# One decay sum made from the other on VectorE from step 3 on, with all instruction orders drawn up anew, in a fused RWKV6 and squared-ReLU kernel

## The chip, the cores and the metric

The kernel runs on one core of a Trainium2 chip. The metric is the device time of one execution in microseconds. Before the change three runs took 183.56, 183.57 and 184.78 us; the median is 183.57.

The engines are named as in the profile: PE is TensorE (matrix products), PEld its weight loads, DVE is VectorE, ACT is ScalarE, POOL is GpSimd, SP is SyncE, which here only issues DMAs. SBUF is the on-chip memory; PSUM is the accumulator memory into which PE writes and which DVE and ACT can read.

## The reference

A recurrence per batch and head, over 768 time steps, then a feed-forward part over its 3072 output rows. Cut to what matters:

```python
# r, k, v, w: (4 batches, 8 heads, 768 steps, 48); u: (8, 48); w_in: (384, 2048); w_out: (2048, 384)
for t in range(S):
    cur = einsum('bhd,bhe->bhde', u[None] * kt, vt)
    y[:, :, t] = einsum('bhd,bhde->bhe', rt, state + cur)
    state = wt[:, :, :, None] * state + einsum('bhd,bhe->bhde', kt, vt)
x = y.transpose(0, 2, 1, 3).reshape(B * S, H * D)      # (3072, 384)
h = x @ w_in
r = maximum(h, 0.0)
out = (r * r) @ w_out
```

## The kernel before

**Tiling.** The 3072 rows are worked off in 12 steps, s = 0 to 11, of 256 time steps each: three per batch, so steps 0, 3, 6 and 9 begin a batch. In a step, partition p holds the time steps 2p and 2p + 1, and the two halves of 64 partitions are two chunks c = 0, 1 of the recurrence. The heads go in four pairs.

**The recurrence of a step.** `ww_` multiplies the decays of the two time steps of a partition, `lw_` takes the logarithm (ACT) into one of two buffers `lw_buf`, in bfloat16. `cum_` forms sums of these logarithms on PE as products with constant triangles: four narrow products with `half_ones` (L309) give each chunk's whole decay, one 384-column product with `tri_strict` (L311) the sum before each time step, and one with `tri_incl_neg` (L312) the negated sum up to and with it. Both 384-column sums stand in one PSUM tile `cs` of two banks, `att0` or `att1`. `exp_` (L317, ACT) takes the exponential of both in place, `ac_` that of the chunk decays. `rd_` (DVE) multiplies r by the first (L332, two instructions) and k by the second (L335); `rw_` and `kw_` have before that multiplied r and k of one of the two time steps by a decay. `tr_` transposes the two on PE and `rkt_` copies them to SBUF (steps 0 to 3), or `dtr_` transposes them by DMA (steps 4 to 11). `p_` (L385) multiplies them, `pm_` (DVE) applies a mask, `y_` (L441) multiplies with v (`vs_`, a rearranged copy; `v_` is another in bfloat16), `su_` (L412) forms the chunk's share of the state, `ts_`, `sn_` and `sb_` pass the state on, `yc_` (L441) adds what comes from the state. `ku_`, `qp_`, `q_`, `qs_` and `vq_` form the part with u, which `ysb_` (L463, DVE) adds to y. The result is transposed by PE (`yt_`) and copied (`xt_`) in steps 0 to 5, and by DMA (`dyt_`) in steps 6 to 11.

**The feed-forward part of a step.** `m1_` in eight groups (L492, 6 products of 256 columns each), each into one of two PSUM banks; `rl_` (ReLU, ACT or DVE) empties the bank; `sq_` squares two groups at a time (ACT or DVE); `m2_` (L517) in two halves of 128 rows, each four parts of four products of 384 columns; `os_` (ACT or DVE) and a store. The weights come as float32 in four pieces each (`ld.*.i`, `ld.*.o`) and are cast once (`cast`).

**The order.** There is no scheduler at run time and none at build time: a string `ORDER` lists every operation, and a loop at the end issues them one by one. The order of the words that fall to one engine is the order of that engine's queue, and each engine works its queue strictly in order, waiting at an instruction until what it reads is written and what it overwrites has been read. A word names the operation, the step, a part, the PSUM bank behind a colon and, where there is a choice, the engine behind an equals sign: `rl_.1.4=A` on ACT, `=V` on DVE, `=G` on POOL. `warm_.9.0` are nine products of a zero tile of 512 columns into a bank that nobody reads (L534), issued where PE has nothing to do in the opening. All loads, stores and DMA transposes stand in SP's queue.

Before, the opening of `ORDER` is:

```
ld.0.w ww_.0=V ld.0.k kw_.0=G lw_.0 warm_.9.0 cum_.0:0 exp_.0 rd_.0.1 warm_.8.1 tr_.0.1:0 rkt_.0.1=A ld.0.r
rw_.0=V ld.1.w ww_.1=G rd_.0.0 warm_.4.2 tr_.0.0:1 ld.0.u ku_.0=V qp_.0=V q_.0 ac_.0 lw_.1 ld.1.k ld.0.v
```

Of the kernel before, what the change touches and what calls it, by code (L numbers as in the profile page):

```python
# [17 lines left out]
ld.0.w ww_.0=V ld.0.k kw_.0=G lw_.0 warm_.9.0 cum_.0:0 exp_.0 rd_.0.1 warm_.8.1 tr_.0.1:0 rkt_.0.1=A ld.0.r  # L18
rw_.0=V ld.1.w ww_.1=G rd_.0.0 warm_.4.2 tr_.0.0:1 ld.0.u ku_.0=V qp_.0=V q_.0 ac_.0 lw_.1 ld.1.k ld.0.v
ld.1.r ld.1.v warm_.1.0 cum_.1:1 rkt_.0.0=A warm_.1.0 p_.0.0:m kw_.1=G ld.2.w pm_.0.0 p_.0.1:0 pm_.0.1 ku_.1=G  # L20
exp_.1 v_.0=A rd_.1.1 rw_.1=G qp_.1=V ld.2.i warm_.7.0 su_.0:m vs_.0.1=A ts_.0.0=A ld.1.i vs_.0.0=A qs_.0=A
ld.0.i sn_.0.0 warm_.5.0 y_.0:0 tr_.1.1:0 sb_.0.0=A warm_.2.1 yc_.0 vq_.0=G ww_.2=G ts_.0.1=V rd_.1.0
rkt_.1.1=V vs_.1.0=A v_.1=A warm_.1.2 tr_.1.0:1 ysb_.0=V lw_.2 rkt_.1.0=V warm_.4.2 yt_.0:0 sn_.0.1 sb_.0.1=A
ac_.1 vs_.1.1=G q_.1 qs_.1=G p_.1.1:0 p_.1.0:m vq_.1=G cast.i.2=A cast.i.1=A xt_.0=V pm_.1.0 su_.1:b ts_.1.0=V
cum_.2:1 sn_.1.0 pm_.1.1 cast.i.0=G m1_.0.4:0 m1_.0.5:1 sb_.1.0=A y_.1:0 yc_.1 ts_.1.1=V rl_.0.5=V ysb_.1=V
rl_.0.4=A m1_.0.2:1 rl_.0.2=A ld.2.k m1_.0.3:0 ld.2.r kw_.2=G rl_.0.3=A exp_.2 ld.3.i yt_.1:0 sn_.1.1
m1_.0.0:1 m1_.0.1:0 cast.i.3=G ld.2.v ku_.2=V xt_.1=V rl_.0.0=A ac_.2 rl_.0.1=A m1_.1.0:1 qp_.2=G rw_.2=V
rl_.1.0=A m1_.1.1:0 rl_.1.1=A sb_.1.1=A ld.0.o m1_.1.3:1 rd_.2.0 rd_.2.1 ld.1.o rl_.1.3=V tr_.2.0:1 cast.o.0=G
tr_.2.1:0 rkt_.2.0=V m1_.1.2:0 m1_.1.6:1 rkt_.2.1=V rl_.1.2=V v_.2=A sq_.0.0=A p_.2.1:0 p_.2.0:1 q_.2 su_.2:b
ts_.2.0=V pm_.2.0 m1_.0.6:0 rl_.1.6=A sq_.0.1=A rl_.0.6=A m1_.0.7:1 rl_.0.7=A ld.2.o vs_.2.1=G vs_.2.0=G  # L30
m2_.0.0.0:0 pm_.2.1 sn_.2.0 sq_.1.0=V m1_.1.4:0 cast.o.1=A cast.o.2=V m2_.0.1.0:1 ld.3.o rl_.1.4=A qs_.2=A
m1_.1.7:1 sb_.2.0=V vq_.2=V cast.o.3=V sq_.0.2=A sq_.1.1=V ld.3.w m2_.0.1.1 m1_.1.5:0 ld.3.k ld.3.r ku_.3=G
y_.2:1 yc_.2 m2_.0.0.1 rl_.1.7=A sq_.0.3=A m2_.0.1.2 m2_.0.0.2 m2_.0.1.3 m2_.0.0.3 ww_.3=V lw_.3 ld.3.v
os_.0.1=A os_.0.0=A cum_.3:0 ysb_.2=V yt_.2:1 xt_.2=V exp_.3 ac_.3 rl_.1.5=V sq_.1.3=A sq_.1.2=A m2_.1.0.0:0
m1_.2.3:1 ld.4.w vs_.3.0=G kw_.3=V qp_.3=V m1_.2.1:0 m2_.1.0.1 rw_.3=G rl_.2.1=A v_.3=A rl_.2.3=A m2_.1.0.2
m2_.1.0.3 ww_.4=G m1_.2.5:0 rd_.3.1 su_.3:1 ld.4.r ld.4.k q_.3 vs_.3.1=A rd_.3.0 m1_.2.4:1 os_.1.0=A qs_.3=G
ts_.3.0=A sn_.3.0 rl_.2.4=V tr_.3.1:1 lw_.4 kw_.4=G tr_.3.0:0 rw_.4=G rkt_.3.1=A cum_.4:0 exp_.4 rl_.2.5=V
m1_.2.0:1 ld.4.v rl_.2.0=A m1_.2.2:0 m2_.1.1.0:1 rl_.2.2=A m2_.1.1.1 ts_.3.1=V rkt_.3.0=V sn_.3.1 rd_.4.1
ku_.4=G vq_.3=G p_.3.0:m v_.4=A ac_.4 sq_.2.2=A sb_.3.0=A rd_.4.0 pm_.3.0 ld.6.w su_.4:1 p_.3.1:0 m2_.1.1.2
m2_.1.1.3 ld.5.k pm_.3.1 m1_.2.6:0 y_.3:0 yc_.3 qp_.4=G sq_.2.1=A sq_.2.0=A m1_.2.7:1 ld.5.w os_.1.1=V  # L40
m2_.2.0.0:0 ts_.4.0=V dtr_.4.1 dtr_.4.0 sb_.3.1=A rl_.2.6=A sn_.4.0 ld.6.v ld.6.k ld.5.r ww_.5=G ysb_.3=V q_.4
yt_.3:1 m2_.2.0.1 ts_.4.1=V m2_.2.0.2 p_.4.1:0 p_.4.0:1 rl_.2.7=V sq_.2.3=V xt_.3=A m2_.2.1.0:1 vs_.4.1=A
lw_.5 m1_.3.2:0 store.1.0 m1_.3.3:1 qs_.4=G pm_.4.1 sn_.4.1 rl_.3.2=A vs_.4.0=G cum_.5:0 m1_.3.0:0 rl_.3.3=A
vq_.4=G sb_.4.0=V pm_.4.0 ac_.5 ww_.6=G m1_.3.7:1 exp_.5 m2_.2.0.3 sq_.3.1=A y_.4:1 rl_.3.0=V rl_.3.7=A yc_.4
ld.6.r rw_.6=G m1_.3.1:0 ku_.5=G qp_.5=G m1_.3.4:1 ld.7.w store.1.1 os_.2.0=A ku_.6=G m2_.2.1.1 kw_.5=V
rw_.5=V kw_.6=V rl_.3.1=A lw_.6 m1_.3.5:0 ld.5.v ysb_.4=V store.2.0 cum_.6:1 ww_.7=G ld.8.w yt_.4:0 ld.7.k
kw_.7=G rd_.5.1 rd_.5.0 xt_.4=V rl_.3.4=A sq_.3.0=A rl_.3.5=A exp_.6 m1_.3.6:1 v_.6=A m2_.2.1.2 rl_.3.6=V
m2_.3.0.0:0 m1_.4.3:0 v_.5=A m2_.2.1.3 ac_.6 su_.5:0 rd_.6.1 rd_.6.0 rl_.4.3=V dtr_.5.0 su_.6:1 ts_.5.0=V
sq_.3.2=A sb_.4.1=A dtr_.5.1 q_.5 sq_.3.3=A os_.2.1=A vs_.5.0=A lw_.7 dtr_.6.0 qs_.5=A vs_.5.1=A ld.7.v ld.7.r
m1_.4.7:1 m1_.4.5:0 rl_.4.5=V m2_.3.0.1 m2_.3.0.2 m2_.3.0.3 m1_.4.6:0 ts_.6.0=V sn_.6.0 sn_.5.0 sb_.5.0=A  # L50
ts_.6.1=V qp_.6=G vs_.6.0=G p_.5.1:0 p_.5.0:1 rl_.4.7=V m2_.3.1.0:1 m1_.4.0:1 rl_.4.6=V pm_.5.1 dtr_.6.1
sq_.4.3=A os_.3.0=A vq_.5=G m2_.3.1.1 rl_.4.0=V pm_.5.0 vs_.6.1=A cum_.7:0 m2_.3.1.2 m1_.4.1:0 y_.5:1 ac_.7
exp_.7 rl_.4.1=A sb_.6.0=A yc_.5 m1_.4.4:1 m2_.3.1.3 q_.6 sq_.4.0=A ysb_.5=V ku_.7=G qp_.7=G rw_.7=G ww_.8=G
yt_.5:0 ld.8.v ld.9.v rl_.4.4=V p_.6.1:1 m1_.4.2:0 xt_.5=V pm_.6.1 ld.9.w rd_.7.1 m1_.5.4:1 m2_.4.1.0:0 v_.7=G
rl_.4.2=A m1_.5.3:0 ld.8.k rd_.7.0 rl_.5.4=A m1_.5.7:1 rl_.5.3=A store.0.0 sn_.6.1 p_.6.0:1 rl_.5.7=V su_.7:0
ld.8.r m1_.5.5:0 ww_.9=G qs_.6=A m1_.5.6:1 pm_.6.0 q_.7 ts_.7.0=V sq_.4.1=A vq_.6=G rl_.5.6=A dtr_.7.0 lw_.8
os_.3.1=V y_.6:1 dtr_.7.1 rl_.5.5=V sn_.7.0 ts_.7.1=V vs_.7.1=G yc_.6 m2_.4.1.1 m1_.5.0:1 m2_.4.0.0:1
vs_.7.0=A rl_.5.0=A v_.9=A ld.9.r m1_.5.2:0 sq_.4.2=V ysb_.6=V kw_.8=V rl_.5.2=A dyt_.6 store.3.0 sb_.6.1=A
sb_.7.0=A cum_.8:0 m2_.4.0.1 sq_.5.1=A store.2.1 store.3.1 m2_.4.0.2 ld.9.k p_.7.0:m p_.7.1:1 pm_.7.0
m2_.4.1.2 m2_.4.0.3 m1_.5.1:0 m2_.4.1.3 m1_.6.7:1 exp_.8 pm_.7.1 qs_.7=G sn_.7.1 vq_.7=G rl_.5.1=A lw_.9  # L60
rw_.8=G rd_.8.0 rd_.8.1 os_.4.0=A m1_.6.2:0 y_.7:1 rl_.6.7=A ac_.8 yc_.7 vs_.8.1=G rl_.6.2=A v_.8=G ld.10.v
rw_.9=G dtr_.8.1 dtr_.8.0 sb_.7.1=V os_.4.1=V cum_.9:0 m1_.6.3:1 sq_.5.2=A sq_.5.0=V exp_.9 rl_.6.3=V
sq_.5.3=A sq_.6.1=A ac_.9 kw_.9=G ku_.9=G ku_.8=G qp_.8=G m1_.6.0:0 m2_.5.0.0:1 m2_.5.0.1 rl_.6.0=V ysb_.7=V
m1_.6.1:1 m1_.6.4:0 m2_.5.0.2 rd_.9.0 rl_.6.4=A rl_.6.1=V store.4.1 m2_.5.0.3 su_.8:1 rd_.9.1 su_.9:0
ts_.8.0=V sn_.8.0 p_.8.0:m dyt_.7 p_.8.1:1 pm_.8.0 m2_.5.1.0:0 ld.10.w m2_.5.1.1 m1_.7.4:0 vs_.8.0=A sq_.6.0=A
m1_.7.0:1 sb_.8.0=A os_.5.0=V q_.8 ts_.9.0=V m2_.5.1.2 m2_.5.1.3 rl_.7.4=A rl_.7.0=V pm_.8.1 m1_.7.7:0
m1_.7.2:1 y_.8:1 ww_.10=V yc_.8 ld.11.w dtr_.9.1 rl_.7.7=A qs_.8=G vq_.8=G rl_.7.2=A m1_.6.5:0 m1_.6.6:1
# [520 lines left out]
```

## Time and profile before

| | us |
|---|---|
| three runs | 183.56, 183.57, 184.78 |
| median | 183.57 |
| the profiled execution | 184.86 |
| its span, first to last instruction | 182.9 |
| outside the span | 1.96 |

| engine | busy us | share of the span | instructions |
|---|---|---|---|
| PE | 173.3 | 95% | 2150 |
| PEld | 124.2 | 68% | 2150 |
| DVE | 141.3 | 77% | 218 |
| ACT | 131.9 | 72% | 237 |
| POOL | 114.4 | 63% | 151 |

The span is what the trace shows of one execution. A row of the timeline has the start, the duration, the engine, the line, the operation with output and input, the count, and in brackets how long the engine had been idle before it and what ended that. A row of the groups has, behind the bar, the busy time, the mean duration of one in ns, and the idle time before them. PE's durations run from the issue of a product to its modelled end, and products overlap: what one takes of PE's time is the distance to the start of the next. A busy share is an average; the stretches differ.

### The profile page before, as it was taken

Reading aid. Unit: us, or ns where it says so; the run is one execution under the profiler, and the core shown is the slowest. Engines: PE = TensorE matmul, PEld = TensorE weight load, DVE = VectorE, ACT = ScalarE, POOL = GpSimd, SP = SyncE. Lnnn points to the kernel's source line nnn. Section 1 sums busy time; section 2 is a strip of 40 time slices with the busy share of each in tenths; the row PEclk is TensorE's granted clock in tenths of the full one; section 3 lists DMA queues with packets and bytes.
Section 4 is the critical chain, followed back from the end, with each engine's and each line's share of the span. In section 5 each row is a group of like instructions: output and inputs, shape, how many; then the busy total and the mean of one; then the engine's idle time right before and its main releaser. Section 6 shows DMA issues by size and latency. Waiting matters only on the chain.

```text
span 182.9 us, 5277 instructions
## 1 busy us (share of the span) xinstructions
PE 173.3 (95%) x2150; PEld 124.2 (68%) x2150; DVE 141.3 (77%) x218; ACT 131.9 (72%) x237; POOL 114.4 (63%) x151
## 2 busy tenths in 40 slices
...
GB/s 141 267 268 303 380 287 345 373 286 236 224 271 142 230 291 292 147 159 199 264 203 167 272 191 189 192 193 282 144 109 87 117 47 88 72 61 86 0 128 90
DMA packets 79208, 35.80 MB, mean 196 GB/s; under 512 B 72400, under 2 KB 77648, under 8 KB 79184
## 3 DMA queue, kind: packets, MB, share of 16 engines
...
## 4 chain that ended last, share of the span: by engine, by line
PE 69%; DVE 8%; ACT 8%; DMA 7%; issue 5%; POOL 1%; DVEq 0%; ACTq 0%; POOLq 0%
PE m L492 28%; PE bk L517 27%; DMA xT<-y_sb 5%; PE att L441 4%; PE bk L534 3%; ACT gt L501 2%; PE att L385 2%; DMA w_raw<-in_w_dram 2%; DVE rdec_buf L332 2%; ACT att L317 2%; DVE gt L503 1%; ACT v_bf L259 1%; DVE y_sb L463 1%; ACT gt L509 1%; POOL ku L302 1%
## 5 line engine op out<-in xcount | busy, mean ns | idle before, releaser
L492 PE MATMUL m<-xT,wi_sb 128*128 128x256 bf16 x576 | 73.9, 273 | 1.3 <-DMA xT<-y_sb 1.0
L517 PE MATMUL bk<-wo_sb,gt 128*128 128x384 bf16 x384 | 71.8, 326 | 0.0
L492 PEld LDWEIGHTS <-wi_sb 128*128 128x128 bf16 x576 | 55.0, 98 | 14.4 <-DMA xT<-y_sb 1.8
L501 ACT ACTIVATE gt<-m 128x512 f16<-128x512 f32 x60 | 35.4, 595 | 22.9 <-PE m L492 22.1
L517 PEld LDWEIGHTS <-gt 128*128 128x128 bf16 x384 | 36.7, 98 | 19.4 <-ACT gt L509 0.2
L509 ACT ACTIVATE gt<-gt 128x1024 bf16<-128x1024 f16 x37 | 38.4, 1053 | 4.1 <-DVE gt L503 3.8
L503 DVE TENSOR_SCALAR gt<-m 128x512 f16<-128x512 f32 x36 | 24.6, 687 | 10.6 <-PE m L492 10.3
L398 DVE TENSOR_TENSOR pmT<-att,mask 128x1024 bf16<-128x1024 f32 x19 | 22.8, 1216 | 0.1
L284 POOL TENSOR_TENSOR ku<-k_raw,u_bc 128x768 f32<-128x768 f32 x10 | 18.5, 1854 | 5.0 <-DMA k_raw<-in_k_dram 5.0
L302 POOL TENSOR_TENSOR ku<-v_sh,qs 128x768 f32<-128x768 bf16 x11 | 16.3, 1479 | 1.9 <-ACT qs L264 1.4
L289 POOL TENSOR_TENSOR ku<-ku,r_raw 128x768 f32<-128x768 f32 x9 | 16.7, 1850 | 0.2
L427 POOL TENSOR_TENSOR S<-t_state,ac_buf 128x192 bf16<-128x192 f32 x20 | 11.7, 588 | 4.1 <-DVE t_state L420 1.8
L264 POOL COPY qs<-q 64x8 f32<-64x8 f32 x32 | 6.3, 196 | 12.8 <-DVE q L293 11.7
L335 DVE TENSOR_TENSOR kdec_buf<-k_raw,att 128x768 bf16<-128x768 f32 x12 | 11.4, 948 | 3.7 <-ACT att L317 2.5
L332 DVE TENSOR_TENSOR rdec_buf<-r_raw,att 128x384 bf16<-128x384 f32 x24 | 12.2, 548 | 1.3 <-ACT ac_buf L322 1.1
L534 PE MATMUL bk<-warm 128*128 128x512 bf16 x33 | 11.9, 510 | 1.2 <-DVE half_ones L220 1.2
L264 POOL CAST v_sh<-v_raw 64x384 bf16<-64x384 f32 x20 | 10.7, 535 | 3.2 <-DMA v_raw<-in_v_dram 2.3
L463 DVE TENSOR_TENSOR y_sb<-att,ku 128x768 bf16<-128x768 f32 x12 | 11.4, 953 | 1.5 <-PE att L441 0.7
L436 ACT COPY sb_buf<-S 64x192 bf16<-64x192 bf16 x32 | 11.1, 346 | 2.0 <-POOL S L427 1.8
L524 ACT ACTIVATE o_sb<-bk 128x384 f32<-128x384 f32 x12 | 5.8, 487 | 8.7 <-PE bk L517 8.1
L277 POOL TENSOR_TENSOR k_raw<-k_raw,w_raw 128x384 f32<-128x384 f32 x8 | 8.7, 1082 | 5.2 <-DMA k_raw<-in_k_dram 5.2
L511 DVE TENSOR_TENSOR gt<-gt 128x1024 bf16<-128x1024 f16 x11 | 7.8, 715 | 5.3 <-ACT gt L501 5.1
...
## 6 DMA issues: line engine op xcount, KB each, us to landing
...
rT<-rdec_buf SPq DMA_TRANSPOSE x16, 3.5
```

Source lines behind the costliest of these rows:

```text
L264: copy(out[j * Q:(j + 1) * Q, c], src[c * Q:(c + 1) * Q, :, j])
L284: tensor_mul("ku_", s)(ku[:], raw["k", s][:, :, 1:3, :], u_bc[:, :, None, :].to_broadcast([C, H, 2, D]))
L289: tensor_mul("qp_", s)(ku[:], ku[:], raw["r", s][:, :, 0:2, :])
L302: tensor_mul("vq_", s)(vq[:], tiles["vs", s][:], tiles.pop(("qs", s))[:, :, :, None].to_broadcast([C, 2, H, D]))
L332: nc.vector.tensor_mul(rdec[0][:, :, j, :, 0:D], x[:, :, j, :].rearrange("p (a e) d -> p a e d", e=2), dec.rearrange("p (a e) d -> p a e d ...
L398: nc.vector.tensor_mul(pmT, ps_p[:].rearrange("p e (x t) -> p (e x) t", x=4), mk.to_broadcast([C, 8, C]))
L492: nc.tensor.matmul(ps1[:, j, :], wi_sb[:, n // 4, kk, n % 4 * 128:(n % 4 + 1) * 128], tiles["xT", s][:, :, kk, :], start=(kk == 0), stop=( ...
L501: nc.scalar.activation(rl, m1, AF.Relu, scale=RS)
L503: nc.vector.tensor_scalar(out=rl, in0=m1, scalar1=RS, scalar2=0.0, op0=ALU.mult, op1=ALU.max)
L509: nc.scalar.activation(gt, rl, AF.Square)
L517: nc.tensor.matmul(m2, gt[:, n, c * C:(c + 1) * C], wo_sb[:, n, :], start=(n == 0), stop=(n == NT - 1))
L534: nc.tensor.matmul((bk + m1_bank)[i][:] if i < 4 else att[i - 4][:, 0, :], warm[:, 0:C], warm[:], start=True, stop=True)
```

## The change

From step 3 on `cum_` leaves out the product with `tri_incl_neg`. The negated inclusive sum is minus the strict sum minus the logarithm itself, and a new operation `al_` forms it so, in one DVE instruction that reads the strict sum from PSUM and the logarithms from SBUF and writes the second bank of the same PSUM tile. `al_` stands in `ORDER` between `cum_` and `exp_`; a step has it where `ORDER` names it (steps 3 to 11). The value that it adds is the bfloat16 logarithm that the product summed too.

```diff
+    ONE_SUM = {int(w.split(".")[1]) for w in ORDER.split() if w.startswith("al_.")}
...
-        nc.tensor.matmul(cs[:, 0, 0:DM], tri_strict[:], lw[:, :, 0:D], start=True, stop=True)
-        nc.tensor.matmul(cs[:, 1, 0:DM], tri_incl_neg[:], lw[:, :, 0:D], start=True, stop=True)
+        nc.tensor.matmul(cs[:, 0, 0:n], tri_strict[:], lw[:, hs, 0:D], start=True, stop=True)
+        if s not in ONE_SUM:
+            nc.tensor.matmul(cs[:, 1, 0:n], tri_incl_neg[:], lw[:, hs, 0:D], start=True, stop=True)
+
+
+    def al_(s):
+        cs, lw = tiles["cs", s], lw_bufs[s % NLW]
+        nc.vector.scalar_tensor_tensor(
+            out=cs[:, 1, 0:DM].rearrange("p (h d) -> p h d", h=H), in0=cs[:, 0, 0:DM].rearrange("p (h d) -> p h d", h=H),
+            scalar=-1.0, in1=lw[:, :, 0:D], op0=ALU.mult, op1=ALU.subtract)
```

`ORDER` is replaced as a whole: the place of nearly every operation on every engine, the bank of many, and the engine of some. The opening, up to the first m1_, has 44 dummy products instead of 42, and eleven instead of nine ahead of `cum_.0`; the loads of step 0 come in another order, and those of later steps stand earlier. Its lines of which the text speaks, the opening up to the first words of step 1's second half, the words around the first m1_, around `al_.3`, and from `yc_.6` on:

```diff
+ld.0.w ld.0.r ld.0.k ld.0.u ld.0.v ld.1.w ld.1.k rw_.0=G ww_.0=V lw_.0 warm_.11.0 cum_.0:0 exp_.0 rd_.0.0
+ld.1.r kw_.0=G ld.1.v warm_.8.1 tr_.0.0:0 ac_.0 ku_.0=G rd_.0.1 rkt_.0.0=V ld.2.i warm_.3.2 tr_.0.1:1 v_.0=A
+rkt_.0.1=V vs_.0.1=A warm_.2.4 su_.0:m qp_.0=V ld.2.w p_.0.0:1 ww_.1=G p_.0.1:0 pm_.0.0 ld.1.i kw_.1=G
+vs_.0.0=A lw_.1 q_.0 ts_.0.0=A warm_.5.0 cum_.1:1 ku_.1=V sn_.0.0 ld.0.i exp_.1 pm_.0.1 rw_.1=G sb_.0.0=A
+ld.2.k ts_.0.1=V qs_.0=A warm_.8.0 y_.0:0 qp_.1=G rd_.1.0 yc_.0 v_.1=A rd_.1.1 warm_.2.1 tr_.1.0:0 vs_.1.0=A
+vq_.0=G q_.1 warm_.1.2 tr_.1.1:1 su_.1:m ac_.1 rkt_.1.0=A rkt_.1.1=V ld.2.r sn_.0.1 ysb_.0=V cast.i.2=A
+vs_.1.1=G p_.1.0:1 ld.3.i ts_.1.0=V p_.1.1:0 pm_.1.0 yt_.0:0 sn_.1.0 ww_.2=G xt_.0=A ts_.1.1=V pm_.1.1
+sb_.0.1=A warm_.4.1 m1_.0.4:0 qs_.1=G ld.2.v lw_.2 m1_.0.5:1 cast.i.1=V rl_.0.4=A cum_.2:1 rl_.0.5=A y_.1:0
+sb_.1.0=V exp_.2 vq_.1=V yc_.1 ld.0.o m1_.0.3:0 cast.i.0=G sq_.0.2=A ysb_.1=V m1_.0.2:1 rl_.0.3=A ld.1.o
+yt_.1:1 ac_.2 rl_.0.2=A kw_.2=G m1_.0.1:0 xt_.1=V sn_.1.1 m1_.1.5:1 rl_.0.1=A rd_.2.1 ld.2.o ku_.2=G m1_.0.0:0
...
+m2_.1.0.0:0 al_.3 lw_.4 m1_.2.1:0 ld.5.w sq_.1.2=V exp_.3 cum_.4:1 kw_.3=V m1_.2.4:1 ac_.3 rl_.2.1=A ku_.3=V
+m2_.1.0.1 rl_.2.4=A ld.4.v al_.4 rw_.3=G m1_.2.2:0 ac_.4 rd_.3.1 exp_.4 m2_.1.0.2 qp_.3=G ld.6.w rd_.3.0
...
+sn_.7.0 ld.8.r m1_.5.6:1 sb_.6.1=A ku_.8=G store.2.1 m2_.4.1.2 q_.7 rl_.5.7=A y_.6:1 rl_.5.6=A ts_.7.1=V yc_.6
+qs_.7=A m1_.5.4:0 ysb_.6=V vs_.8.0=G m1_.5.2:1 vs_.7.0=A rl_.5.4=V dyt_.6 ww_.8=G p_.7.1:0 p_.7.0:1 rl_.5.2=A
+pm_.7.1 m2_.4.0.0:0 vq_.7=G sb_.7.0=A ld.9.k m1_.5.3:0 pm_.7.0 lw_.8 store.3.1 m1_.5.1:1 ld.9.v qp_.8=G
+cum_.8:0 rl_.5.3=A ld.9.r sq_.5.1=A rl_.5.1=V m2_.4.0.1 al_.8 y_.7:1 ld.10.r ww_.9=V yc_.7 exp_.8 kw_.8=G
+m1_.5.5:0 ysb_.7=V lw_.9 m1_.6.6:1 sq_.4.3=A ld.10.w rl_.5.5=V rw_.8=G m2_.4.0.2 rl_.6.6=V sq_.5.0=A cum_.9:1
```

The code around it gains further forms of the operations that this `ORDER` does not use: half a step at a time (an argument `h`, `c` or `f`), and another layout of the masked products (`SPREAD`, `sp_`), for which two small constant tiles are reserved but not filled. What the instructions of the unchanged operations do is as before.

406 lines of the change are left out of this document (231 added, 175 removed).

## The prediction

> **What bounds the kernel now.** I read the profile by stretches of time first, cut where the stage changes: up to the first product of the feed-forward part, its first ten microseconds, the long middle, the part after the recurrence has run out of vector work, with PE, PEld, DVE, ACT and POOL busy in that order, then the granted clock and the DMA share.
>
> ```profile
> 0.00:23.70 23.70, 20.44 (x246) 10.05 (x247) 17.86 (x31) 15.89 (x33) 16.06 (x34) 1.00 1.06 272
> 23.70:33.00 9.30, 8.87 (x104) 7.61 (x104) 8.28 (x14) 7.93 (x15) 8.17 (x7) 1.00 1.09 325
> 33.00:113.00 80.00, 77.42 (x1105) 57.50 (x1104) 70.16 (x109) 69.03 (x128) 62.99 (x73) 1.00 1.11 228
> 113.00:174.20 61.20, 61.20 (x668) 46.00 (x667) 44.40 (x66) 36.60 (x60) 27.22 (x39) 1.00 0.56 116
> ```
>
> From 23.7 us on TensorE is the bound: it is idle 2.6 us of the 80 in the middle and not at all from 113 to 174.2. DVE (70.2 of 80, 88%) and ACT (69.0, 86%) have little room in the middle and plenty after it. So three things can change the time: what TensorE has to do after its first real product, when that product comes, and how often the middle makes it wait. The waits of TensorE are few:
>
> ```profile
> PE m L492 <- DMA xT<-y_sb: 1.0, 2, 0.6
> PE att L412 <- DVE rdec_buf L332: 0.8, 1, 0.8
> PE att L385 <- DVE rdec_buf L332: 0.6, 1, 0.6
> ```
>
> That is 2.4 us: two transposes by DMA that landed late, and two steps whose decayed r came late from VectorE. Before 23.7 us TensorE does mostly dummies, and the chain there runs through VectorE.
>
> **The second decay sum, steps 3 to 11.** One 384-column product (L312) goes, and al_ comes on VectorE between the first product and exp_.
>
> ```profile
> 44.27 0.32 PE L311 MATMUL att<-lw_buf,tri_strict 128*128 128x384 bf16 x1
> 44.44 0.32 PE L312 MATMUL att<-lw_buf,tri_incl_neg 128*128 128x384 bf16 x1
> 44.60 0.50 PE L472 MATMUL bk<-ident,y_sb 128*128 128x128 bf16 x6
> ```
>
> A product shows 0.32 us, but the next one starts 0.16 us later; the rest is pipeline. What TensorE saves is the start-to-start time: 9 x 0.16 = **1.45 us**. The whole 0.32 would make 2.9 us; I take it as the far end only, since these rows show the neighbours overlapping.
>
> al_ reads 384 float32 columns of PSUM and 384 columns of lw and writes PSUM. No such instruction is in the trace. The nearest rows:
>
> ```profile
> L332 DVE TENSOR_TENSOR rdec_buf<-r_raw,att 128x384 bf16<-128x384 f32 x4 | 2.0, 548 | 0.0
> L289 DVE TENSOR_TENSOR ku<-ku,r_raw 128x768 f32<-128x768 f32 x2 | 1.9, 955 | 0.0
> L335 DVE TENSOR_TENSOR kdec_buf<-k_raw,att 128x768 bf16<-128x768 f32 x2 | 1.9, 950 | 2.5 <-ACT att L317 2.5
> L293 DVE TENSOR_REDUCE q<-ku 128x16 f32<-128x768 f32 x2 | 1.9, 948 | 0.0
> L398 DVE TENSOR_TENSOR pmT<-att,mask 128x1024 bf16<-128x1024 f32 x1 | 1.2, 1216 | 0.0
> ...
> L463 DVE TENSOR_TENSOR y_sb<-att,ku 128x768 bf16<-128x768 f32 x1 | 1.0, 957 | 0.1
> L284 DVE TENSOR_TENSOR ku<-k_raw,u_bc 128x768 f32<-128x768 f32 x1 | 0.9, 950 | 0.0
> L362 DVE COPY kT<-bk 128x1024 bf16<-128x1024 bf16 x1 | 0.7, 685 | 0.0
> ...
> L422 DVE TENSOR_TENSOR t_state<-S,att 128x192 f32<-128x192 bf16 x3 | 1.1, 352 | 0.0
> ```
>
> It lies between 0.35 us (L422, half the columns) and 0.95 us (L335, twice the columns); L332 has its width, one PSUM and one SBUF input, so I take 0.55 and 9 x 0.55 = 5.0 us of VectorE (3.2 to 8.6). On the path I cost it at nothing: counted in the order with the start-to-start times that stand further below, 9 to 17 us of other products lie between a step's cum_ and its first p_. The cover can fail in two ways. al_ waits for cum_ in VectorE's queue, and behind it wait that engine's rl_ and sq_; exp_ waits for al_ on ACT, and behind exp_.3 wait ac_.3 and rl_.2.1, which frees a bank that m1_ needs. If al_ is late, TensorE stops at the next m1_, and each such case costs about what L332's waits cost now, 0.6 to 0.8 us. lw_ of step s+2 writes the buffer that al_ of step s reads, but several products stand between.
>
> **Load of the vector engines.** VectorE pays for al_ by giving up three vs_ (two instructions each), five os_, two qp_ and two kw_, and gets two casts, two rl_, an rw_ and a vq_; by the means of their rows that is 0.5 us less over the kernel. ACT gains: three more v_, two more vs_ (two instructions each) and five os_, for two casts less.
>
> ```profile
> L264 ACT CAST v_sh<-v_raw 64x384 bf16<-64x384 f32 x14 | 7.1, 507 | 0.1
> ...
> L259 ACT CAST v_bf<-v_raw 128x768 bf16<-128x768 f32 x6 | 4.9, 832 | 0.0
> ```
>
> The v_ and vs_ alone are 3 x 0.83 + 4 x 0.51 = 4.5 us, against ACT's 11.0 us of idle time in the middle. It fits, with less room.
>
> **The opening.** The loads go w, r, k, u, v instead of w, k, r, w, u, k; eleven dummies stand ahead of cum_.0 instead of nine.
>
> ```profile
> 1.19 4.02 PE L534 MATMUL bk<-warm 128*128 128x512 bf16 x9 [1.19 <-DVE half_ones L220]
> 5.93 0.26 PE L309 MATMUL att<-half_ones,lw_buf 128*128 128x2 bf16 x4 [0.72 <-ACT lw_buf L252]
> ...
> 6.65 3.62 PE L534 MATMUL bk<-warm 128*128 128x512 bf16 x8
> 10.06 0.76 PE L346 MATMUL bk<-ident,kdec_buf 128*128 128x128 bf16 x8
> 10.65 1.03 PE L534 MATMUL m<-warm 128*128 128x512 bf16 x4
> ```
>
> A dummy takes (10.06 - 6.65)/8 = 0.43 us early and about 0.22 us in the row at 10.65, though the granted clock reads 1.00 throughout. The first run of dummies, 4 us and then a break of 0.72 us, did not bring the fast rate; the second, unbroken from 5.93 to 10.06, did. Eleven dummies at 0.43 fill 1.19 to 5.9, just where lw_.0 is done, so cum_.0 is not later and TensorE never pauses. I take it that the rate then doubles after some 4.1 unbroken us, before cum_.0 is over. The eight dummies behind it end near 8.4 instead of 10.06, and tr_.0.0 waits for VectorE, not for TensorE. The Trainium skill (TensorE: Matmul & The Clock Gate, "Part 1: The HAM clock gate") has half rate until one fully busy window of 3.4 us has passed, with windows that run freely. The two runs above fit that; it puts the doubling between 4.6 and 8.0 us, and at the late end tr_.0.0 would come 0.2 us later, the opening gaining 0.4 instead of 0.6 us.
>
> ```profile
> 4.69 0.56 DVE L248 TENSOR_TENSOR ww<-w_raw 128x384 f32<-128x384 f32 x1 [1.04 <-DMA w_raw<-in_w_dram]
> ...
> 6.89 0.80 ACT L317 ACTIVATE att<-att 128x768 f32<-128x768 f32 x1 [1.02 <-PE att L312]
> ...
> 9.18 1.01 POOL L248 TENSOR_TENSOR ww<-w_raw 128x384 f32<-128x384 f32 x1 [1.86 <-DMA w_raw<-in_w_dram]
> ```
>
> The fourth load lands at 9.18, the first at 4.69: 1.5 us each. So r is there at 6.2, k at 7.7, v (behind half-sized u) at 9.9, the next k at 12.9: all but k ahead of their use, and k holds rd_.0.1 by some 0.15 us. From exp_.0's end on VectorE paces both kernels. Before, it needs 16.0 us of instructions by their durations to the end of xt_.0 and takes 14.9 (7.78 to 22.69), a ratio of 0.935. Now up to ysb_.0: four rd_ products of L332 (2.2), two L335 (1.9), three copies (2.1), qp_, two q_, ku_, ysb_ (4.8), two pm_ (2.4), ts_ (0.35), together 13.7; times 0.935 is 12.8; with 0.4 us of waits for k and tr_ it ends at 21.0. Then yt_ (0.50, as at 44.60) and its copy by ACT (0.80, as L317 for 768 columns): the first m1_ stands near 22.3, where it was
>
> ```profile
> 23.70 1.48 PE L492 MATMUL m<-xT,wi_sb 128*128 128x256 bf16 x12
> ...
> 29.68 1.47 PE L492 MATMUL m<-xT,wi_sb 128*128 128x256 bf16 x12 [0.26 <-ACT ac_buf L322]
> ```
>
> So 1.4 us earlier. But cum_.2 now stands behind it (0.4 us), and so do VectorE's cast of the input weights and sb_.1.0, on which yc_.1 waits:
>
> ```profile
> L436 DVE COPY sb_buf<-S 64x192 bf16<-64x192 bf16 x6 | 1.9, 321 | 0.0
> L190 DVE CAST wo_sb<-w_st 128x1536 bf16<-128x1536 f32 x2 | 1.9, 953 | 0.0
> ```
>
> 0.95 + 2 x 0.32 = 1.6 us behind the last pm_.1, of which y_.1 covers 0.4: about 1.2 us of waiting with what follows at yt_.1. Before has some 0.8 us of gaps between the two rows above. The opening gives 1.4 - 0.4 - 0.4 = **0.6 us**. If the fast rate comes no earlier than at 10.06, everything is 1.0 us later, and the opening loses 0.4.
>
> **Waits in the middle.** The new order puts more between a product and its use: from a step's transposes (dtr_) to its p_ there are 4 to 10 us of other products, where step 9 had 1.3 and step 4 had 1.6. The loads stand earlier too: w of step 4 goes ahead of k, r and v of step 3, which costs these 1.5 us each by the spacing above, covered by the 11 us between ld.3.k and its rd_. The tightest place I find is step 6. From yc_.6 to m1_.6.6 there are five m1_, two m2_, p_.7, the shorter cum_.8 and y_.7 with its yc_:
>
> ```profile
> 62.25 0.58 PE att L385 x32
> ...
> 66.63 0.65 PE bk L517 x4
> 67.28 0.74 PE att L441 x24
> 68.03 0.67 PE m L492 x6
> ```
>
> 7 x 0.65 + 0.58 + 0.27 + 0.74 = 6.1 us, against ysb_ (0.95) and a transpose
>
> ```profile
> xT<-y_sb SPq DMA_TRANSPOSE x6, 3.8
> ```
>
> of 3.8 us: it holds unless VectorE is more than 1.4 us behind. Of the 2.4 us I let 2.0 stay: **0.4 us** gained, between all of it and the same again lost. The last 32 products, the copy and the store are as long as before.
>
> **Sum.** The profiled execution took 184.86 us (span 182.9), 1.3 above the median of 183.57. Against its own time: 184.86 - 1.45 - 0.6 - 0.4 = 182.4; by the median 183.57 - 2.45 = **181.1 us**.
>
> **Rivals.** *The middle runs out of vector time (slower).* Against the first 64 m1_ groups the new lists put some 2.6 us more on VectorE and 6 us more on ACT, while TensorE has 0.7 us less there. Their idle time in the middle is 9.8 and 11.0 us, so both would be above 90% busy, and al_ adds a place where the two queues wait for each other. It decides once each al_ holds a queue that an m1_ needs: nine waits of the L332 size (0.72) in place of two, 7 x 0.72 = 5.0 us, which gives 183.57 - 1.45 - 0.6 + 5.0 = 186.5. For it speaks the load; against it that the 88% of VectorE come with two waits only, and the longer distances. 0.20. *Only the products go (within 1%).* The fast rate comes at 10.06 as now, the waits stay: 183.57 - 1.45 + 0.4 = 182.5; 183.3 with another 0.8 us wait. 0.25. *All waits go.* 183.57 - 1.45 - 0.6 - 2.4 = 179.1. 0.13. That the change does not do what it says is out: nine products fewer and nine al_ stand in the lists.
>
> **Chances.** The forecast has 0.42, its own range 180.0 to 182.4. One per cent of 183.57 is 1.8 us, about what a measurement can tell: the line is 181.7. Of the forecast 0.32 lie below it and 0.10 above. Faster 0.32 + 0.13 = 0.45, within 1% 0.25 + 0.10 = 0.35, slower 0.20. The range 178.9 to 185.6 takes in all cases but the upper part of the slow one.
>
> **What would show it.** Right: first m1_ near 22.3; the second run of dummies at 0.22; al_ at 0.55; 2 us of waits on TensorE from 33 to 113 and none after. Wrong: dummies at 0.43 until 10; al_ near 0.95; TensorE waiting at m1_ for rl_, or at p_ for rdec_buf, in most of steps 3 to 9.

## The result, and the profile after

Four runs of the changed kernel took 189.81 to 193.21 us, median **191.18**, beside 183.94 for the kernel before (four runs, 183.56 to 184.78). Some runs of a kernel are disturbed and longer by some per cent, so from here on a time is the median of the runs that are at most 1.5% above the fastest of their kernel, and a count such as 3 of 4 says how many of its runs these are. For the changed kernel this is **190.77** (3 of 4), 6.8 us more than before. The ratio is 1.036, with a 95% interval of 1.028 to 1.044: slower. The forecast was 181.1, the range ended at 185.6. The profiled execution took 191.58 us, its span is 189.2 (before 182.9).

The same stretches of the changed kernel, columns as before:

```profile
0.00:23.70 23.70, 20.24 (x253) 10.62 (x254) 18.58 (x31) 15.82 (x33) 19.18 (x36) 1.00 1.02 272
23.70:33.00 9.30, 7.78 (x93) 6.30 (x92) 7.74 (x9) 6.64 (x13) 8.73 (x7) 1.00 1.05 314
33.00:113.00 80.00, 75.36 (x1016) 55.53 (x1015) 71.83 (x107) 69.38 (x131) 61.10 (x66) 1.00 1.03 220
113.00:174.20 61.20, 58.36 (x713) 43.64 (x711) 44.18 (x66) 41.99 (x75) 27.01 (x38) 1.00 0.62 130
```

TensorE is idle 4.6 us of the 80 in the middle (before 2.6), 2.8 us of the stretch after it (before none) and 1.5 us of the nine before it (before 0.4). By the page, PE is busy 173.1 of 189.2 us, where it was 173.3 of 182.9: its idle time grew by 6.5 us and the span by 6.3. So the work did not get longer; TensorE waits. The waits of PE by what ended them (total, times, longest):

```profile
PE att L502 <- ACT sb_buf L497: 1.5, 1, 1.5
PE att L473 <- ACT v_bf L288: 1.3, 1, 1.3
PE bk L606 <- DVE wo_sb L201: 1.3, 1, 1.3
PE bk L623 <- DVE half_ones L233: 1.2, 1, 1.2
PE att L502 <- DVE sb_buf L497: 1.1, 1, 1.1
```

No engine stands out: ACT, VectorE, copies of v, a cast of weights, the state. Such a list suggests that something which feeds all of them is late; for the cast of weights (`wo_sb`) another reason is shown below. The opening, in PE's timeline:

```profile
1.19 4.88 PE L623 MATMUL bk<-warm 128*128 128x512 bf16 x11 [1.19 <-DVE half_ones L233]
...
6.51 1.89 PE L623 MATMUL bk<-warm 128*128 128x512 bf16 x8
8.24 0.22 PE L395 MATMUL bk<-ident,rdec_buf 128*128 128x128 bf16 x1
...
22.54 1.47 PE L581 MATMUL m<-xT,wi_sb 128*128 128x256 bf16 x12
26.09 0.33 PE L502 MATMUL att<-sb_buf,rT 128*128 128x96 bf16 x4 [1.08 <-DVE sb_buf L497]
...
28.14 0.51 PE L561 MATMUL bk<-ident,y_sb 128*128 128x128 bf16 x6 [0.41 <-DVE y_sb L551]
```

The eight dummies behind `cum_.0` take (8.24 - 6.51)/8 = 0.22 us each, the first m1_ stands at 22.54, and behind it come 1.08 + 0.41 us of waits. And the new operation, from the groups:

```profile
L354 DVE SCALAR_TENSOR_TENSOR att<-att,lw_buf 128x384 f32<-128x384 f32 x9 | 5.0, 557 | 0.2 <-PE att L347 0.2
```

What differs most from the kernel before is the last column but one of the windows, the mean busy share of the DMA engines (above 1 where packets of one engine overlap in the records). The kernel before, cut finer:

```profile
33.00:50.00 17.00, 16.93 (x212) 12.38 (x213) 15.32 (x24) 15.55 (x27) 8.98 (x12) 1.00 1.01 275
50.00:70.00 20.00, 19.41 (x314) 14.88 (x303) 17.67 (x29) 17.19 (x32) 17.17 (x25) 1.00 1.09 238
...
70.00:90.00 20.00, 19.15 (x260) 14.37 (x259) 16.52 (x25) 17.65 (x35) 17.90 (x16) 1.00 1.10 203
90.00:113.00 23.00, 21.93 (x344) 15.87 (x342) 20.65 (x34) 18.63 (x36) 18.94 (x23) 1.00 1.20 204
```

The changed kernel, with three microseconds by themselves:

```profile
33.00:50.00 17.00, 15.29 (x185) 11.03 (x184) 16.17 (x22) 14.86 (x27) 6.99 (x8) 1.00 1.13 297
50.00:70.00 20.00, 19.79 (x309) 14.64 (x308) 19.25 (x31) 18.65 (x39) 17.52 (x16) 1.00 0.84 187
57.00:60.00 3.00, 3.00 (x77) 1.91 (x76) 3.00 (x6) 2.90 (x9) 2.86 (x6) 1.00 0.05 10
70.00:90.00 20.00, 19.78 (x267) 14.79 (x266) 18.89 (x33) 18.23 (x34) 19.16 (x26) 1.00 0.97 198
90.00:113.00 23.00, 20.50 (x262) 15.07 (x260) 17.53 (x25) 17.64 (x33) 17.42 (x18) 1.00 1.15 210
```

Share times length, added up from 33 to 113 us: before 17.2 + 21.8 + 22.0 + 27.6 = 88.6 us of DMA work done, after 19.2 + 16.8 + 19.4 + 26.5 = 81.9. At 113 us the changed kernel is 6.7 us of DMA work behind by this share. By bytes, the last column, it is less: 18.2 MB before and 17.6 after in these 80 us, 0.6 MB or one and a half loads of 384 KB. From 57 to 60 us its DMA engines stand almost still (0.05). SP's queue shows why; the changed kernel:

```profile
51.01 1.39 SPq L179 DMA_DIRECT2D k_raw<-in_k_dram  x1
58.52 1.34 SPq L424 DMA_TRANSPOSE kT<-kdec_buf  x1
59.97 2.53 SPq L422 DMA_TRANSPOSE rT<-rdec_buf  x2
```

and the kernel before at the same place:

```profile
50.80 1.20 SPq L168 DMA_DIRECT2D w_raw<-in_w_dram  x1
54.40 1.76 SPq L371 DMA_TRANSPOSE kT<-kdec_buf  x1
```

The transposes of step 4 stand ahead of further loads and wait for `rd_.4.1` on VectorE. That holds the queue for 2.4 us before and for 6.1 us (52.40 to 58.52) after, long enough for the engines to run dry. But the windows also show extra idle time of TensorE ahead of this hole: from 33 to 50 us it is idle 1.7 us, where it was 0.1.

### The profile page after: what moved, and what is told of

It is laid out like the page before. It is cut to its first block, busy times and chain, and to the rows that moved or that the text cites. A ratio compares the mean times of both kernels' runs of the same rounds, so it can differ in the third digit from the quotient of the medians.

```text
span 189.2 us, 5286 instructions
## 1 busy us (share of the span) xinstructions
PE 173.1 (91%) x2143; PEld 123.3 (65%) x2143; DVE 144.4 (76%) x213; ACT 137.3 (73%) x255; POOL 116.0 (61%) x144
## 4 chain that ended last, share of the span: by engine, by line
PE 43%; DVE 16%; ACT 15%; DMA 11%; POOL 5%; issue 5%; SPq 3%; DVEq 0%
PE m L581 19%; PE bk L606 18%; ACT gt L590 4%; ACT gt L598 3%; DMA xT<-y_sb 3%; DMA k_raw<-in_k_dram 3%; DMA v_raw<-in_v_dram 3%; DVE pmT L461 3%; DMA w_raw<-in_w_dram 2%; DVE kdec_buf L382 2%; ACT v_sh L293 2%; POOL ku L313 2%; ACT v_bf L288 2%; PE att L502 2%; DVE gt L592 1%
## 5 line engine op out<-in xcount | busy, mean ns | idle before, releaser
L590 ACT ACTIVATE gt<-m 128x512 f16<-128x512 f32 x58 | 33.8, 595 | 13.5 <-PE m L581 12.8
L592 DVE TENSOR_SCALAR gt<-m 128x512 f16<-128x512 f32 x38 | 25.9, 687 | 16.0 <-PE m L581 15.5
L461 DVE TENSOR_TENSOR pmT<-att,mask 128x1024 bf16<-128x1024 f32 x22 | 26.2, 1217 | 1.7 <-PE att L442 1.6
L318 POOL TENSOR_TENSOR ku<-ku,r_raw 128x768 f32<-128x768 f32 x11 | 20.0, 1816 | 6.4 <-DVE ku L313 3.9
L613 ACT ACTIVATE o_sb<-bk 128x384 f32<-128x384 f32 x17 | 8.3, 486 | 14.6 <-PE bk L606 7.4
L337 POOL TENSOR_TENSOR ku<-v_sh,qs 128x768 f32<-128x768 bf16 x10 | 14.8, 1477 | 0.8 <-ACT v_sh L293 0.7
L293 ACT CAST v_sh<-v_raw 64x384 bf16<-64x384 f32 x26 | 13.2, 509 | 1.0 <-DMA v_raw<-in_v_dram 0.7
L280 POOL TENSOR_TENSOR ww<-w_raw 128x384 f32<-128x384 f32 x8 | 8.6, 1069 | 5.8 <-DMA w_raw<-in_w_dram 5.5
L288 ACT CAST v_bf<-v_raw 128x768 bf16<-128x768 f32 x11 | 9.1, 830 | 4.0 <-DMA v_raw<-in_v_dram 3.9
L323 DVE TENSOR_REDUCE q<-ku 128x16 f32<-128x768 f32 x12 | 11.3, 945 | 0.5 <-POOL ku L318 0.4
```

Of the source, the lines that this page charges most:

```text
L288: copy_on("v_", s)(v_bf[:].rearrange("p j (h d) -> p h j d", h=H), raw["v", s][:])
L293: copy(out[j * Q:(j + 1) * Q, c], src[c * Q:(c + 1) * Q, :, j])
L318: tensor_mul("qp_", s, h)(ku, ku, raw["r", s][:, heads(h), 0:2, :])
L337: tensor_mul("vq_", s)(vq[:], tiles["vs", s][:], tiles["qs", s][:, :, :, None].to_broadcast([C, 2, H, D]))
L461: nc.vector.tensor_mul(pmT, ps_p[:].rearrange("p e (x t) -> p (e x) t", t=w), mk.to_broadcast([C, 4 * n, w]))
L590: nc.scalar.activation(rl, m1, AF.Relu, scale=RS)
```

## The experiments

Two theories. **DMA**: up to some 130 us the DMA engines are a second bound, just below TensorE; the new order leaves them idle for a while, has TensorE run the recurrence ahead of what they deliver, and TensorE pays. **VectorE's queue** (the rival of the prediction): al_ holds VectorE, and what stands behind it is late. The ratios are to the kernel before on the same chip.

| kernel | us (runs counted) | before there | ratio, 95% interval |
|---|---|---|---|
| before's order, al_ behind cum_ | 189.69 (1 of 4) | 185.14 | none |
| before's order, al_ ahead of exp_ | 189.11 (3 of 5) | 184.42 | 1.026, 1.011 to 1.041 |
| changed, al_ left out | 187.87 (1 of 4) | 185.14 | none |
| changed, a v load earlier | 190.04 (3 of 4) | 185.14 | 1.032, 1.020 to 1.043 |
| changed, stores earlier | 193.49 (4 of 4) | 185.14 | 1.046, 1.037 to 1.054 |
| before's order, opening of the changed one | 186.15 (4 of 4) | 184.76 | 1.011, 1.004 to 1.018 |
| before, 6 loads more | 190.52 (1 of 4) | 184.76 | none |
| before, v and w loads cut | 183.96 (10 of 10) | 184.76 | 0.997, 0.992 to 1.001 |
| changed, v and w loads cut | 183.34 (8 of 10) | 184.76 | 0.994, 0.989 to 0.999 |
| changed, cut, al_ left out | 182.71 (8 of 11) | 184.42 | 0.992, 0.987 to 0.997 |
| before's order, al_ behind cum_, cut | 193.18 (5 of 5) | 184.42 | 1.051, 1.042 to 1.059 |
| changed, first hole filled | 189.67 (3 of 5) | 184.69 | 1.028, 1.019 to 1.036 |
| the same without al_ | 187.88 (5 of 5) | 184.69 | 1.020, 1.013 to 1.027 |
| before with such a hole | 186.13 (4 of 5) | 184.69 | 1.010, 1.000 to 1.021 |
| changed, two holes filled | 189.86 (4 of 5) | 183.42 | 1.031, 1.022 to 1.040 |
| the same without al_ | 189.05 (5 of 5) | 183.42 | 1.026, 1.018 to 1.034 |

### Which part of the change: al_ alone, the order alone, the opening alone

al_ put into the order of the kernel before, right behind each cum_:

```diff
-cum_.3:0 ysb_.2=V yt_.2:1 xt_.2=V exp_.3 ac_.3
+cum_.3:0 al_.3 ysb_.2=V yt_.2:1 xt_.2=V exp_.3 ac_.3
...
-vs_.4.0=G cum_.5:0 m1_.3.0:0
+vs_.4.0=G cum_.5:0 al_.5 m1_.3.0:0
```

> The order of before, untouched, with al_ right behind cum_ in steps 3 to 11 and the second product left out there. If the new orders made the loss (late loads and stores in SP's queue, longer queues), al_ alone keeps about its price of the prediction: 183.9 - 1.45 = 182.5 us, a ratio of 0.985 to 0.998. If al_ made it, by the load on VectorE and by queues that wait for each other, nine waits of 0.5 us or more come in: 187 us or more, a ratio above 1.015.

189.69 us by the one run that counts, 4.6 more than the kernel before there. Its VectorE timeline around the first al_:

```profile
43.34 0.57 DVE L354 SCALAR_TENSOR_TENSOR att<-att,lw_buf 128x384 f32<-128x384 f32 x1 [1.53 <-PE att L347]
43.81 0.95 DVE L551 TENSOR_TENSOR y_sb<-att,ku 128x768 bf16<-128x768 f32 x1
```

al_.3 waits 1.53 us for cum_.3, `ysb_.2` behind it is late by that, and TensorE waits 1.59 us at yt_.2. So the queue theory holds here, from the first al_ on; in all, VectorE waits 4.8 us at four al_ for their cum_. The changed order without al_ (both products back on TensorE):

```diff
-m2_.1.0.0:0 al_.3 lw_.4 m1_.2.1:0
+m2_.1.0.0:0 lw_.4 m1_.2.1:0
```

> The order of after without al_, both sums by products in every step. If al_ made the loss, it goes: 185 to 187 us, with 5 us less on VectorE. If the orders made it, TensorE pays 1.45 us more and the waits stay: 190 to 193 us.

187.87 us, again one run, 2.7 more than the kernel before and between the two expectations. So either half seems to lose by itself, 4.6 us for al_ in the old order and 2.7 for the new order without al_; with one run each, neither size is firm. The opening of the changed kernel (its words up to the first m1_) with the rest of the order before:

> The opening of after up to the word ahead of its first m1_, then every other word in the order of before (no al_, no dummies behind). If what the opening gains stays, 1.0 us less than before: 182.6 us, with dummies at 0.22 us from some 6 us on. If DMA paces the middle, the gain is given back there: 183.5 to 185 us. If orders do not bear being joined, more waits: 186 us or more.

186.15 us against 184.76. Its timeline of PE shows that this does not measure the opening cleanly, since the seam costs:

```profile
20.55 0.65 PE L441 MATMUL att<-rT,kT 64*64 64x128 bf16 x32 [1.38 <-ACT rT L409]
23.76 0.25 PE L344 MATMUL att<-half_ones,lw_buf 128*128 128x2 bf16 x4 [1.26 <-DVE pmT L460]
```

Its first m1_ comes at 24.20 and not at 22.54; what an opening 1.2 us shorter is worth stays open.

### Single waits of the changed kernel

The 1.28 us wait for `v_bf` at 92.98 hangs on a load of v that SP issued late, so the load changed places with another:

```diff
-cum_.5:0 ld.7.r ld.8.v m1_.3.3:1
+cum_.5:0 ld.7.r ld.7.v m1_.3.3:1
...
-m2_.3.0.3 ld.7.v lw_.7
+m2_.3.0.3 ld.8.v lw_.7
```

> The order of after with the words ld.7.v and ld.8.v exchanged, so that v of step 7 is loaded two transposes and some 22 us earlier and v of step 8 later. If late words in SP's queue cost the time, the 1.28 us wait at 92.98 and the small ones behind it up to 98.6 go: 1.5 to 2.5 us less than after, about 189 us. If the vector engines are simply full, another wait takes its place: 191 us as after.

190.04 us, and a ratio of 1.032 where the changed kernel has 1.036: no gain clear of noise. In the trace, of a run of 192.88 us, the wait is gone from the list of PE's waits, and another stands at its head:

```profile
PE att L442 <- DMA rT<-rdec_buf: 4.9, 5, 2.0
PE bk L606 <- DVE wo_sb L201: 1.3, 1, 1.3
```

There five waits for DMA transposes stand in place of one for a load; whether the shorter runs have them too is not shown. Stores of steps 2, 3 and 4 moved ahead, so that the output buffers come free earlier:

```diff
-ku_.8=G store.2.1 m2_.4.1.2
+ku_.8=G store.2.1 store.2.0 m2_.4.1.2
...
-rl_.11.1=V store.2.0 m2_.10.1.2
+rl_.11.1=V m2_.10.1.2
```

> The order of after with store.2.0, store.3.0 and store.4.0 each moved right behind store.2.1, store.3.1 and store.4.1. If the missing output buffer costs the time, ACT's 3.05 us of waiting for a store at 120.95 goes and with it TensorE's 1.50 us at 122.3: 1.5 to 2.5 us less than after, about 189 us. If ACT is full anyway: 191 us as after.

193.49 us, above both expectations. This too puts DMAs ahead of transposes, and TensorE waits five times for a transposed r, 3.5 us in all, the longest time 1.67 us at 127.26.

### Is it the DMA engines?

In both orders, with every word of SP's queue where it was, the loads of v and w of steps 6 to 11 fetch one head of eight into a tile of four steps earlier; the other heads of these steps hold older data, so that part of the output is left out:

```diff
-        if (part, s) not in raw:
+        if part in "vw" and s >= 6:
+            raw[part, s], h = raw[part, s - 4], 2
+        elif (part, s) not in raw:
             raw[part, s] = a_in.tile([C, H, n, D], FP32, name=f"{part}_raw")
-        t, hs = raw[part, s], heads(h)
+        t, hs = raw[part, s], slice(0, 1) if h == 2 else heads(h)
```

> The kernel after, in which the v and w loads of steps 6 to 11 fetch one head of eight into the tiles of four steps earlier, whose other heads are used again; every word keeps its place in every queue. Left out: the other seven heads' v and w of these steps. 12 x 7/8 x 1.5 us = 16 us of DMA time go. If the DMA engines pace the recurrence and the new order runs ahead of them, most of TensorE's waiting behind 60 us goes: 184 to 186 us. If only the order of words in the queues makes the waits, those for v and w go and the rest stays: 188 to 190 us.

> The kernel before with the same thin loads of v and w in steps 6 to 11, and the same part left out. It has 2.4 us of waits in the middle, so by either theory it gains at most these: 181.5 to 184 us.

The changed kernel falls from 190.77 to **183.34** us, the kernel before from 184.76 to 183.96. With the cut the new order is thus 0.6 us ahead of the old one, with intervals that overlap, where the forecast for the change was 2.45 us. The middle of the changed kernel with the cut loads:

```profile
33.00:113.00 80.00, 78.86 (x1117) 58.36 (x1115) 73.95 (x112) 72.97 (x140) 66.57 (x76) 1.00 0.95 198
```

TensorE waits 1.1 us there instead of 4.6, while VectorE and ACT are busier than ever (74.0 and 73.0 of 80): these two were not its limit.

Not all of this difference is due to the cut. SP issues the first cut load at 48.35 us, and between 23.7 and 50 us TensorE is idle 0.6 us in this trace and 3.2 in the changed kernel's, 0.5 in the kernel before's. The wait of 1.25 us for `wo_sb` at 45.58 is a part of it. VectorE works there on two other products first, in the changed kernel

```profile
41.72 1.52 DVE L337 TENSOR_TENSOR ku<-v_sh,qs 128x768 f32<-128x768 bf16 x1
43.17 1.48 DVE L600 TENSOR_TENSOR gt<-gt 128x1024 bf16<-128x1024 f16 x1
```

beside two products of GpSimd, which start when w has landed,

```profile
41.25 1.18 POOL L280 TENSOR_TENSOR ww<-w_raw 128x384 f32<-128x384 f32 x1 [0.75 <-DMA w_raw<-in_w_dram]
42.80 1.30 POOL L280 TENSOR_TENSOR ww<-w_raw 128x384 f32<-128x384 f32 x1 [0.36 <-DMA w_raw<-in_w_dram]
```

and with the cut loads, where GpSimd starts these at 41.40:

```profile
39.74 0.96 DVE L339 TENSOR_TENSOR ku<-v_sh,qs 128x768 f32<-128x768 bf16 x1
40.62 0.68 DVE L602 TENSOR_TENSOR gt<-gt 128x1024 bf16<-128x1024 f16 x1
```

In eight of ten traces of the new order, with and without the cut, TensorE is idle 2.7 to 4.0 us in this stretch, and in each of the eight one of the two products or the cast behind them takes 1.48 us or more; in the other two (0.6 and 0.7 us) none takes over 0.96. Behind 50 us the cut tells: up to 174.2 TensorE is idle 1.6 and 1.0 us in the two traces of the new order with the cut, and 3.1 to 7.4 in the eight with full loads. The counter-test, the kernel before with six more loads of 384 KB that nobody reads:

```diff
+        if part == "v" and 4 <= s < 10:
+            nc.sync.dma_start(out=junk[0][:].rearrange("p h j d -> p h (j d)"),
+                in_=src[b, hs, i * T:(i + 1) * T, :].rearrange("h (p j) d -> p h (j d)", j=2))
```

> The kernel before with one more load of 384 KB behind each v load of steps 4 to 9, into a tile that nobody reads; nothing is left out. 6 x 1.5 = 9 us more of DMA time. If the DMA engines are a second bound up to 130 us, 5 to 9 us are lost: 189 to 193 us. If they have room and TensorE alone binds, it stays within 1.5 us: 184 to 185.5 us.

190.52 us by the one run of four that counts, against 184.76: 5.8/6 = 0.96 us for each load, about two thirds of the 1.5 us that one load takes of the DMA engines. Its middle:

```profile
33.00:113.00 80.00, 72.34 (x984) 53.38 (x974) 62.90 (x98) 63.41 (x119) 58.17 (x69) 0.98 1.09 246
```

Between 50 and 130 us TensorE is idle 7.9 us there, where it was 2.5. So the kernel before stood close to the balance of TensorE and the DMA engines: less DMA work gained it 0.8 us at most (the interval of its ratio takes in no gain at all), more cost it about two thirds of its DMA time.

### Does the same hold for al_ in the old order?

> The order of the kernel before with the copy-product al_ right behind cum_ in steps 3 to 11, and with the v and w loads of steps 6 to 11 cut to one head of eight (the rest of these tiles holds an earlier step's data, so those steps' output is left out). With full loads this kernel without the cut took about 7 us more than the kernel before. If the DMA engines turn small holds into lost time, most of that goes with the cut: 182.5 to 185.5, against 183.96 for the kernel before with the same cut; the 1.6 us at the transpose of y of step 2 stays, since it falls ahead of step 6. If it is the 9 x 0.56 us of vector time or the place in VectorE's queue alone, whatever the DMA does, it stays near 189 to 191.

193.18 us, 8.8 more than before there: nothing came back, so here the DMA theory falls. Three instructions of VectorE (`kw_.5`, `rw_.5`, `kw_.6`) tell the story. In the order before with the cut loads:

```profile
65.46 0.57 DVE L307 TENSOR_TENSOR k_raw<-k_raw,w_raw 128x384 f32<-128x384 f32 x1
65.95 0.55 DVE L303 TENSOR_TENSOR r_raw<-r_raw,w_raw 128x384 f32<-128x384 f32 x1
66.42 0.55 DVE L307 TENSOR_TENSOR k_raw<-k_raw,w_raw 128x384 f32<-128x384 f32 x1
66.89 0.96 DVE L552 TENSOR_TENSOR y_sb<-att,ku 128x768 bf16<-128x768 f32 x1
```

With al_ in it:

```profile
66.74 0.57 DVE L356 SCALAR_TENSOR_TENSOR att<-att,lw_buf 128x384 f32<-128x384 f32 x1 [1.23 <-PE att L349]
...
70.08 0.98 DVE L308 TENSOR_TENSOR k_raw<-k_raw,w_raw 128x384 f32<-128x384 f32 x1
70.99 2.16 DVE L304 TENSOR_TENSOR r_raw<-r_raw,w_raw 128x384 f32<-128x384 f32 x1
73.08 2.15 DVE L308 TENSOR_TENSOR k_raw<-k_raw,w_raw 128x384 f32<-128x384 f32 x1
75.15 0.94 DVE L553 TENSOR_TENSOR y_sb<-att,ku 128x768 bf16<-128x768 f32 x1
```

al_ waits 1.23 us for its cum_ and takes 0.57; pushed back, the three products no longer run in the one stretch in which GpSimd is idle (65.6 to 66.5 in the other trace) but beside products of GpSimd, two of them long:

```profile
70.61 2.13 POOL L315 TENSOR_TENSOR ku<-k_raw,u_bc 128x768 f32<-128x768 f32 x1
72.82 2.00 POOL L320 TENSOR_TENSOR ku<-ku,r_raw 128x768 f32<-128x768 f32 x1
```

They take 5.1 us instead of 1.4, `ysb_.5` behind them comes late, and TensorE pays:

```profile
76.15 0.24 PE L347 MATMUL att<-half_ones,lw_buf 128*128 128x2 bf16 x4 [3.00 <-DVE y_sb L553]
```

The Trainium skill (SBUF — State Buffer, "Who interferes with whom") has a VectorE instruction with two SBUF inputs contend with a GpSimd instruction that reads SBUF, and one with at most one SBUF input, outside the two-port modes, not. The rows agree: the products of two SBUF tiles go from 0.55 to 2.16 us, while al_, with one input in PSUM, took 0.57 also at 66.74, beside a GpSimd product of 1.48 us.

al_ moved to right ahead of each exp_, so that nothing is pushed back that was ahead of exp_:

```diff
-cum_.3:0 al_.3 ysb_.2=V yt_.2:1 xt_.2=V exp_.3 ac_.3
+cum_.3:0 ysb_.2=V yt_.2:1 xt_.2=V al_.3 exp_.3 ac_.3
```

> The order of the kernel before with al_ in steps 3 to 11, now standing right ahead of exp_ in each step, so that nothing stands behind it on VectorE that was ahead of exp_ before (step 3: the copy of y of step 2 and the gather of xT come first again). If the place in VectorE's queue makes the cost, most of the 7 us that al_ behind cum_ cost goes: 183 to 186. If any hold of 0.56 us ahead of the decayed copies is enough, since it delays the transposes and loads behind them in the DMA queue and that time isn't made up, it stays at 188 to 193. If al_ is worth its products in this order, 182.

189.11 us, 4.7 more than before there, as much as the 4.6 of al_ behind cum_: so the place alone does not seem to make the cost. TensorE now has waits for xT (2.2 us in three) and for the decayed r (1.6).

In the new order al_ has been given its place. There, with room on the DMA engines:

> The changed kernel without al_ (the second decay product is back on TensorE) and with the v and w loads of steps 6 to 11 cut to one head of eight (output of those steps left out). With room on the DMA engines, if the products are worth what the trace says (9 x 0.16 us of TensorE), it takes 183.65 + 1.45 = about 185. If al_ on VectorE costs as much as it saves, it takes 183 to 184. If al_ costs more than it saves even with that room, under 183.

182.71 without al_, 183.34 with it. The intervals overlap, but the gain of 1.45 us that the nine products should be worth is not there.

### The holes of the issuing queue

Three loads moved ahead of the transposes of step 4, where the queue stood still; with al_ and without it:

```diff
-rkt_.3.0=A ld.5.k tr_.3.1:0
+rkt_.3.0=A ld.5.k ld.5.v ld.6.k ld.6.r tr_.3.1:0
```

> The changed kernel with the loads of v of step 5 and of k and r of step 6 moved in the order from behind the transposing DMAs of step 4 to right ahead of them. In the changed kernel's trace the issuing queue stands idle from 52.40 to 58.52 us behind the first of these transposes (it waits for the decayed keys on VectorE), and the DMA share of 57 to 60 us is 0.05. If that hole is the loss (some 4 us of DMA time that is never made up, since the DMA engines are full until some 130 us), 187 to 188. If it is made up later, or the loss lies in VectorE's queue, 190 to 192. If the transposes, now behind three more loads, are what counts, slower than 192.

> The same three loads moved, and al_ left out (both decay products on TensorE). The changed kernel without al_ took 191.0, as long as with it. If the hole is the loss, 187 to 188 here too; if al_ costs a little by itself, as with the cut loads (182.85 without it, 183.65 with it), up to 1 us less than the run with al_. If the hole isn't the loss, 190 to 192.

189.67 and 187.88 us. With al_ that is 1.1 less than without the move, and by ratios to the kernel before (1.028 and 1.036) the intervals overlap; without al_ it is just the 187.87 of the one run without the move. So filling this hole brings little or nothing. The kernel before with two loads moved behind the transposes of step 4, which makes its hole 5.0 us long:

```diff
-rd_.4.0 pm_.3.0 ld.6.w su_.4:1 p_.3.1:0 m2_.1.1.2 m2_.1.1.3 ld.5.k
+rd_.4.0 pm_.3.0 su_.4:1 p_.3.1:0 m2_.1.1.2 m2_.1.1.3
...
-dtr_.4.1 dtr_.4.0 sb_.3.1=A
+dtr_.4.1 dtr_.4.0 ld.6.w ld.5.k sb_.3.1=A
```

> The kernel before with its loads of w of step 6 and k of step 5 moved from ahead of the transposing DMAs of step 4 to right behind them, so that its issuing queue stands idle for some 5 us there (2.4 us before). If a hole of this kind isn't made up, the time goes up by about the two loads' DMA time, 2 x 1.5 = 3 us: 186.5 to 188 where the kernel before takes 183.6 to 185. If it is made up, within 1 us of the kernel before.

186.13 against 184.69: 1.4 us lost, about half of the two loads; the interval of the ratio begins at 1.000. With the first hole filled, the next one stood at 70 us, ahead of the transposes of step 5. Three more loads moved ahead of these:

```diff
-sn_.4.1 ld.7.k m1_.3.6:0 ac_.5
+sn_.4.1 ld.7.k ld.7.v ld.8.w ld.8.k m1_.3.6:0 ac_.5
```

> As the run with three loads moved ahead of the transposes of step 4 (189.75), and the loads of v of step 7 and of w and k of step 8 moved ahead of the transposes of step 5 as well, where that run's issuing queue stood idle from 70.32 to 73.82 us and the DMA share fell to 0.6 to 0.8 between 75 and 84 us. If such holes are the loss, another 2 to 3 us go: 186.5 to 188. If the time lost to DMA only moves on to the next place, 189 to 190.5. If the loads now stand in the way of the transposes, over 190.5.

> The same six loads moved, al_ left out. With three loads moved it took 187.88. If the holes are the loss, 185 to 186.5 (the kernel before: 183.6 to 185.3); if the loss only moves on, 187.5 to 188.5; if the loads stand in the way of the transposes, more.

189.86 and 189.05: nothing more. In the timeline of the former TensorE waits for a transpose of step 4, which stands behind the first three loads:

```profile
66.95 0.21 PE L442 MATMUL att<-rT,kT 64*64 64x128 bf16 x1 [2.69 <-DMA rT<-rdec_buf]
```

With one hole filled and no al_ the same wait is 2.52 us, so it comes with the first move. Loads ahead of a transpose make the transpose late; a transpose ahead of loads makes a hole. In these runs moving words in one full queue shifted the loss; only fewer bytes took it away.

## Why the prediction was wrong, step by step

**What bounds the kernel: this step failed.** The prediction took TensorE as the bound from 23.7 us on and let three things change the time. The DMA share in its own quoted row of the middle, 1.11, was given no weight, and no rival spoke of it. The runs show it as a second bound: 0.96 of 1.5 us per added load reach the end (one run), and cutting 12 loads takes 7.4 us from the changed kernel, a part of which may be the early stretch, and 0.8 from the one before. So the 2.45 us forecast as gained became 6.8 lost. A smaller part of the loss lies ahead of all this: between 23.7 and 50 us TensorE is idle 2.7 us more than before, of which 1.25 us is the wait behind the cast of `wo_sb`, for which the prediction had no term.

**Waits in the middle: failed by the same omission.** That the earlier load "costs these 1.5 us each by the spacing above, covered by the 11 us between ld.3.k and its rd_" counted each load's delay against products of TensorE, not against a queue that was full. "Of the 2.4 us I let 2.0 stay": by the windows, TensorE is idle 4.6 + 2.8 + 1.5 = 8.9 us between 23.7 and 174.2, where it was 2.6 + 0.4 = 3.0. The prediction measured distances in the order in products of TensorE; the new order has longer ones there, but the loads did not come any faster.

**The second decay sum: sizes right, worth wrong.** al_ took 557 ns where 550 was said. "On the path I cost it at nothing" failed: in the old order it costs 4.6 and 4.7 us with full loads and some 9 with the cut ones, as VectorE's queue waits for cum_ at al_ and what follows is pushed beside GpSimd; in the new order the kernels with al_ took 0.6 to 1.8 us more than those without in three pairs, with intervals that overlap in each, and 2.9 more in a fourth that rests on one run. Nowhere did the 1.45 us appear as a gain.

**Load of the vector engines: right for ACT, wrong for VectorE.** ACT went from 131.9 to 137.3 us (4.5 more were said for v_ and vs_ alone). VectorE was to have 0.5 us less and got 3.1 more, 141.3 to 144.4: the means of rows did not hold in the new places. The copies of the state (`sb_`) take 493 ns on average instead of 290, the products of two SBUF tiles in `rw_` 1039 instead of 750. With the cut loads both are busier still in the middle, while TensorE hardly waits.

**The opening: right in its steps.** The fast rate came behind eleven unbroken dummies, in time for the next eight at 0.22 us; the first m1_ stands at 22.54 (said 22.3), with 1.5 us of waits behind it (said 1.2). By the Trainium skill (TensorE: Matmul & The Clock Gate, "Part 1: The HAM clock gate") the prediction estimated the doubling between 4.6 and 8.0 us, and the row at 6.51 lies inside. The 0.6 us are gone by 33 us: TensorE is idle 1.5 us of the last nine, where it was 0.4, and has 58 products of m1_ behind it, where it had 57 and a transpose of step 2 more.

**The rivals.** The slow one came nearest by its time, 186.5, and is still 4.3 us short. It named the queue that al_ holds in the old order, but not the cause here: it asked for nine waits at al_, and the trace of the changed kernel has al_ waiting 0.2 us in all. No rival had the DMA engines in it.

**What stays open.** Which DMA of the new order is the costly one: filling one hole gives 1.1 us of the 6.8 with al_ and none without, filling two no more. How much of the 6.8 us is the early stretch is not measured, since no run kept VectorE and GpSimd apart there; that the two products are long because they run beside GpSimd is read from ten traces. That TensorE waits because the new order runs the recurrence ahead of the DMA is argued from the share of the windows; no run moved the recurrence alone. None of the versions beat the kernel before; those that leave loads out and have no al_ in the old order are at most 1% below it.
